# First part's plain values loaded as f32 on two other queues, plain heads first, and the first FFN tiles split by rows of x

## The chip, the cores and the metric

The kernel runs on one core of a Trainium2 chip. The metric is the device time of one execution in microseconds (us), given as the median of ten runs. One further execution was recorded by the hardware profiler; its rows are what this document reads. Five engines work side by side, each through its own queue of instructions in order: TensorE (PE, with its weight loads shown as PEld), VectorE (DVE), ScalarE (ACT), GpSimd (POOL) and SyncE (SP). Loads and stores (DMAs) are issued by an engine's queue and carried out by 16 DMA engines.

## The reference

Windowed attention over 8 batches, 8 heads, 576 tokens and 64 dimensions, followed by a feed-forward network (FFN) on the 4608 rows that it gives:

```python
scores = scale * np.matmul(q, k.transpose(0, 1, 3, 2))
rel = pos[:, None] - pos[None, :]
mask_plain = (rel >= 0) & (rel < 32)
mask_dil = (rel >= 0) & (rel < 128) & (rel % 4 == 0)
masks = np.stack([mask_plain if h < H // 2 else mask_dil for h in range(H)], axis=0)
attn = softmax(np.where(masks, scores, -1e9))
x = np.matmul(attn, v)            # (8, 8, 576, 64) -> rows of 512
h = np.maximum(x @ w_in, 0.0)     # 512 -> 2048
out = h * h @ w_out               # 2048 -> 512
```

Heads 0 to 3 are the *plain* heads (a window of 32 tokens), heads 4 to 7 the *dilated* ones (every fourth token of 128). Inputs and output are f32 in DRAM.

## The kernel before

**Pairs and parts.** Two heads share the 128 partitions, so there are four pairs e: 0 and 1 are plain, 2 and 3 dilated. The first two batches are worked in two *parts*: part 0 is tokens 0 to 255, part 1 the other 320. Only batch 0 (the "first" steps) and the first FFN tiles matter for the change.

**An order by hand.** The string PROGRAM (line 21) lists what is issued, in order. Everything up to the first bar runs before the first FFN group, what stands between two bars runs after one FFN group each. The engines follow this order each for its own instructions. The codes:

- `L0:q001` loads q and k of batch 0, part 0, pairs 0 and 1 (two DMAs, q then k); `q023` pairs 2 and 3; `q101`, `q123` the same for part 1. `L0:v0d` loads part 0's values of the dilated pairs (tile vds, two DMAs of 64 KB), `L0:v0p` those of the plain pairs (tile vbd, four DMAs of 32 KB as written), `v1dr` and `v1p` the values of part 1. `L0:i0` to `i3` load the four column pieces of w_in, `o0` to `o3` the four pieces of w_out, 512 KB each as written. `L1:...` are the loads of batch 1. All of these are issued by POOL and cast f32 to bf16 on the way. Loads by POOL use eight semaphores in turn, so each issue waits until the load eight before it has landed.
- `T` transposes q and k of a pair on PE (tiles of the PSUM pool ps_a, two buffers), `C` copies the result to SBUF (letter a: ACT takes q, or both; letter v: DVE; the plain pairs' k is always DVE's).
- `B` writes the mask as a large negative bias into a PSUM tile of the pool ps_f (four buffers), `S` adds the scores to it, `E` is the exponential on ACT.
- `P` multiplies the exponentials with the values, `D` sums them, `L` and `X` on ACT make the reciprocal of the sum (Ln, then Exp of its negative), `M` on DVE (line 620) writes the normalized result to xT. In part 0 a pair of pairs shares one L, X and M: `L20 X20 M20` is for pairs 2 and 3, `L00 X00 M00` for pairs 0 and 1.
- `W` and `w` are dummy matmuls on zeros (tile idle, line 465).

**vbd and its zeros.** vbd holds the values of a pair as a block diagonal: head 0's 64 columns on partitions 0 to 63, head 1's on 64 to 127, zeros elsewhere. ACT writes the zeros at the start (line 725), after it has issued the load of the constants mk (line 714); the loads of `v0p` fill the blocks.

**The FFN.** `ffn_groups` (line 645) makes the groups. Four tiles of 256 tokens come first (tile 0: tokens 0 to 255, tile 1: 256 to 511), then tiles of 512. A first-product step mm1(u, kts) multiplies the listed quarters kt of xT (kt is the pair e) with two of the 16 column blocks of w_in, accumulates in a tile of ps_f, and after the last quarter ACT applies Relu (line 679) and DVE squares (line 680). Blocks u = 0, 1 need i0, u = 2, 3 i1, u = 4, 5 i2, u = 6, 7 i3. In tile 0 each group is a whole mm1 of eight matmuls, in the order of quarters 2, 3, 0, 1; so the dilated pairs are wanted first. The *early* tiles (the four after tile 0) split their first groups: tile 1 works half of the quarters for u = 0 to 3 first and the others after, the rest three and one. The second product, `g2` (line 692), runs over tiles of 128 rows and four pieces of w_out, four matmuls a group; ACT copies the result to a tile osb (pool of three buffers) and SP stores it.

Line 808 sets the order of the first 16 groups. In `head`, 0 to 7 are tile 0's first-product groups, 16 to 23 tile 1's; before the change they run 0, 1, 2, 3, 16, 17, 18, 19, 4, 5, 20, 21, 6, 7, 22, 23. The next eight groups are tile 0's second product, pieces o0 and o1 of both row tiles, then o2 and o3.

Of the kernel before, what the change touches and what calls it, by code (L numbers as in the profile page):

```python
# [18 lines left out]


PROGRAM = (
    "L0:q001 L0:q023 L0:q101 L0:q123 L0:v0d L0:v0p L0:i0 L0:v1dr L0:i1 L0:v1p L0:i2 L0:i3 L0:o0 L0:o1 L0:o2 "
    "L0:o3 L1:q00123 z y L1:v0dp L1:q10123 L1:v1dpr w9 T00 C00a T10 C10a B00 B10 S00 E00 B20 S10 E10 B30 T20q "
    "B01 W2 T20k C20v T30 C30v B11 W1 S20 E20 W1 S30 E30 T01 C01v T11 C11v W1 S01 E01 T21 C21v B21 S11 E11 T31 "
    "C31v P20 P30 D20 D30 L20 X20 M20 P00 P10 D00 D10 L00 X00 M00 B31 S21 E21 S31 E31 W2 | | P21 P31 D21 D31 "
    "L21 X21 M21 L31 X31 M31 | | P01 P11 D01 D11 L01 X01 M01 L11 X11 M11 | | | | | | | | | | | | | m n | | | | "
    "| L2:q00123 L2:q10123 | 1q1 1q3 | 1q2 1k2 | 1k1 1v3 | 1a2 | 1v2 1k0 1q0 | 1o2 | 1a0 1a1 | 1k3 1o0 1o1 | "
    "1a3 1Q0 | 1K0 1o3 | 1Q1 1K1 | 1Q2 | 1b0 | | 1Q3 1K2 L2:vwpdr L3:q00123 L3:q10123 | L2:x | | 2q0 | | 2k0 "
# [35 lines left out]
def kernel(  # L64
# [9 lines left out]
    nc = tc.nc  # L74
    P = nc.NUM_PARTITIONS
    B, H, S, D = q.shape
    DM, DFF = moe_w_in.shape
# [3 lines left out]
    f32 = mybir.dt.float32  # L81
# [11 lines left out]
    NT = 512  # L93
# [7 lines left out]
    NF = DFF // P  # L101
# [7 lines left out]
    osb_pool = ctx.enter_context(tc.tile_pool(name="osb", bufs=3))  # L109

    ps_f = ctx.enter_context(tc.tile_pool(name="ps_f", bufs=4, space=bass.MemoryType.PSUM))
    ps_a = ctx.enter_context(tc.tile_pool(name="ps_a", bufs=2, space=bass.MemoryType.PSUM))
    ps_o = ctx.enter_context(tc.tile_pool(name="ps_o", bufs=1, space=bass.MemoryType.PSUM))
# [27 lines left out]
    idle = const.tile([P, 256], bf16, name="idle")  # L141
    kbd = const.tile([P, NE, NB, P], bf16, name="kbd")
    vbd = [const.tile([P, NE, NB, P], bf16, name=f"vbd{i}") for i in range(2)]
# [311 lines left out]
    first = {}  # L455
    sides = [slice(64 * hl, 64 * hl + 64) for hl in range(2)]

    def turn(n: int, cols: int):


        if "W" not in first:
            pool, nm = (ps_f, "pf") if ("P", 2, 0) in first else (ps_o, "po")
            first["W"] = pool.tile([P, 512], f32, name=nm)
        for _ in range(n):
            nc.tensor.matmul(
                first["W"][:, 0:cols], idle[:, 0:P],
                idle[:, 0:256].unsqueeze(1).broadcast_to([P, cols // 256, 256]), start=True, stop=True, skip_group_check=True
            )

    def first_step(code: str):  # L470
# [5 lines left out]
        what, e, part = code[0], int(code[1]), int(code[2])  # L476
        m0, n = MS[part], MN[part]
# [81 lines left out]
        elif what == "E":  # L559
            ps = first.pop(("S", e, part))  # L560
            nc.scalar.activation(pts[e][:, c : c + ps.shape[1]], ps, ACT.Exp, scale=SCALE)
        elif what == "P":
            if ("P", *pair) not in first:
                if pair in ((2, 0), (2, 1), (0, 1)):
                    od = ps_o.tile([P, 512], f32, name="po"), ps_d.tile([P, 512], f32, name="pd")
                else:
                    od = [ps_a.tile([P, 512], f32, name="pa") for _ in range(2)]
                first.pop("W", None)
                first["P", *pair] = od
            o, d = [x[:, y0 : y0 + w] for x in first["P", *pair]]  # L570
            o3, d3 = byr(o), byr(d)
            pt = pts[e]
            bl = blocks(0, e, part)
            y, dms = c, []
            for x, (i, r, q0, q1) in enumerate(bl):
                z = (q1 - q0) * (RES if r is None else 1)
                quads = dil and i < 8
                for rows in sides if quads else [slice(0, P)]:
                    if r is None:
                        to, rhs = o3[rows, :, q0 - m0 : q1 - m0], byr(pt[rows, y : y + z])  # L580
                    else:
                        to, rhs = o3[rows, r, q0 - m0 : q1 - m0], pt[rows, y : y + z]
                    if quads:
                        lhs = vds[0][rows, e - NE // 2, i // RES, D * (i % RES) : D * (i % RES) + D]
                    else:
                        lhs = vbd[0][:, e, i, :]
                    nc.tensor.matmul(
                        to, lhs, rhs, start=(x == 0 and y0 == 0), stop=(x == len(bl) - 1), skip_group_check=True
                    )
                if not dil:  # L590
                    dms.append((d3[:, :, q0 - m0 : q1 - m0], byr(pt[:, y : y + z])))
                y += z
            if dil and part == 0:
                dms.append((d, pt[:, 0:w]))
            elif dil:
                main = byr(pt[:, c : c + 448])
                dms += [(d3, main[:, :, 32:112]), (d3[:, :, 0:32], main[:, :, 0:32]),
                        (d3[:, :, 64:80], byr(pt[:, c + 448 : c + 512]))]
            first["D", e, part] = dms
        elif what == "D":  # L600
            dms = first.pop(("D", e, part))
            for x, (dd, rh) in enumerate(dms):
                nc.tensor.matmul(
                    dd, ones, rh, start=(x == 0 and y0 == 0), stop=(x == len(dms) - 1), skip_group_check=True
                )
        else:
            n = 512 if part == 0 else w
            if what == "L":
                first["X", e, part] = rec = r_pool.tile([P, 512], f32, name="rec")
                nc.scalar.activation(rec[:, 0:n], first["P", e, part][1][:, 0:n], ACT.Ln)  # L610
            elif what == "X":
                rec = first["X", e, part][:, 0:n]
                nc.scalar.activation(rec, rec, ACT.Exp, scale=-1.0)
            else:
                o, rec = first["P", e, part][0][:, 0:n], first.pop(("X", e, part))[:, 0:n]
                to = xT[:, e, RES * m0 : RES * m0 + n]
                if part == 0:
                    to = xT[:, e : e + 2, 0:w]
                    o, rec = [x.rearrange("p (e n) -> p e n", e=2) for x in (o, rec)]
                nc.vector.tensor_tensor(out=to, in0=o, in1=rec, op=ALU.mult)  # L620
# [24 lines left out]
    def ffn_groups(tk0: int, nt: int):  # L645

        early = 0 < tk0 <= 2 * NT
        h2 = h2_pool.tile([P, NF, NT], bf16, name="h2T")  # L650
        per = NT // nt
        kts = (0, 2, 1, 3) if tk0 >= NT else (2, 3, 0, 1)
        cut = 3 if tk0 >= NT else 2
        cur, acc = {}, {}

# [24 lines left out]
            nc.vector.tensor_tensor(out=hv, in0=hv, in1=hv, op=ALU.mult)  # L680

        def g1(i):
            if i < 2 and early:
                for u in (2 * i, 2 * i + 1):
                    mm1(u, kts[:cut])
            elif i < 4 and early:
                for u in (2 * i - 4, 2 * i - 3):
                    mm1(u, kts[cut:])
            else:
                mm1(i, kts)  # L690
# [21 lines left out]


    nc.scalar.dma_start(mk[:, :], mk_dram.ap())

    def zero_halves(t):
        nc.vector.memset(t[0:64, :, :, 64:128], 0.0)
# [49 lines left out]
    def run(code):  # L767
        if code == "y":
            for nm in "qk":
                nc.gpsimd.memset(staged(1, nm)[64:80, 0, :, :], 0.0)  # L770
                nc.gpsimd.memset(staged(2, nm)[64:80, 0, 0 : H // 2, :], 0.0)
        elif code == "z":
            nc.gpsimd.memset(vbd[1][0:64, :, :, 64:128], 0.0)
            nc.gpsimd.memset(vbd[1][64:128, :, :, 0:64], 0.0)
        elif code == "m":
            masks()
        elif code == "n":
            zero_halves(kbd)
            zero_halves(vbd[0][:, NE // 2 :, 0:8, :])
        elif code[0] in "wW":  # L780
            turn(int(code[1:]), 512 if code[0] == "w" else 256)
        elif code[0] in "TCBSEPDXM" or code[0] == "L" and code[2:3] != ":":
            first_step(code)
        elif code[0] != "L":
            step(int(code[0]), code[1:])
        else:
            b, what, part, which = int(code[1]), code[3], code[4:5], code[5:]
            if what == "q":
                load_qk(b, None if part == "w" else int(part), [int(e) for e in which])
            elif what == "x":  # L790
                cross_all(b)
            elif what == "v":
                load_v(b, [0, 1] if part == "w" else [int(part)], which)
            else:
                (load_w_in if what == "i" else load_w_out)(int(part))
# [9 lines left out]
        groups += ffn_groups(tk0, nt)  # L805

    head = groups[:G]
    groups[:NF] = [head[y] for y in (0, 1, 2, 3, 16, 17, 18, 19, 4, 5, 20, 21, 6, 7, 22, 23)]
    groups[NF:G] = [head[y] for y in (8, 9, 12, 13, 10, 11, 14, 15)] + head[24:32]
    for b in range(5, B):  # L810
        at = {"a": (-2, 8), "b": (0, 8), "o": (3, 8), "p": (6, 8), "v": (-4, 8)}
# [51 lines left out]
```

## Time and profile before

| what | value |
|---|---|
| median of 10 runs | 314.42 us (313.24 to 351.95) |
| the profiled execution | 313.35 us, of which the span of its instructions is 311.3 us |
| PE busy | 300.3 us (96%), 2532 matmuls |
| DVE busy | 193.9 us (62%) |
| ACT busy | 196.7 us (63%) |
| POOL busy | 96.5 us (31%) |
| first product, L668 | 132.7 us |
| second product, L700 | 131.1 us |
| granted TensorE clock | 1.00 |

The time counts a little more than the span of the instructions. Busy time of an engine says how much of the span it had an instruction running; what an engine waits for is read from the chain of waits and from the rows in order of time, where square brackets give the idle time ahead of an instruction and what ended it. In the windows view each engine has its busy time and a count of instructions, then come the granted clock, the mean busy share of the 16 DMA engines (over 1 when packets overlap) and GB/s. A row of the DMA queues gives packets, MB and the share of 16 engines over the span.

PE and the 16 DMA engines over the span, in 40 equal slices (the busy share in tenths):

```profile
PE   8889999999999999999999999999999999999994
DMA  7999999999999969999699976502200210121022
```

### The profile page before, as it was taken

What the parts mean: (1) busy time and instruction counts of PE and PEld (TensorE: products, weight loads), DVE (VectorE), ACT (ScalarE), POOL (GpSimd) and SP (SyncE); (2) the same over time, 40 slices, a digit from 0 to 9 for tenths busy, and PEclk for the clock granted to TensorE, in tenths of its full rate; (3) what the DMA queues carried; (4) which work ended last, traced back from release to release, by engine and by line L of the source; (5) the groups of instructions that cost most, each with busy time, mean ns of one, the idle gap of its engine ahead of it and who ended that gap; (6) DMA issues with size and microseconds to landing.
All of it is one profiled execution on the core that took longest, in us unless ns stands there. A gap on an engine that the chain in (4) does not pass through costs nothing.

```text
span 311.3 us, 6742 instructions
## 1 busy us (share of the span) xinstructions
PE 300.3 (96%) x2532; PEld 186.3 (60%) x2564; DVE 193.9 (62%) x631; ACT 196.7 (63%) x420; POOL 96.5 (31%) x142
## 2 busy tenths in 40 slices
PE   8889999999999999999999999999999999999994
PEld 3679746968755555565599555555555555445443
DVE  1435667998978879974898469946994334104400
ACT  7377738859878865785388547854786456226511
POOL 8889783665227255501451041000000000000000
PEclk9999999999999999999999999999999999999999
DMA  7999999999999969999699976502200210121022
GB/s 111 161 165 212 205 153 151 183 157 206 150 106 189 182 109 203 156 100 198 99 134 130 159 119 92 101 10 61 67 2 1 69 68 0 36 67 34 0 69 67
DMA packets 79808, 34.91 MB, mean 112 GB/s; under 512 B 49824, under 2 KB 74784, under 8 KB 79776
## 3 DMA queue, kind: packets, MB, share of 16 engines
q0 software_dynamic: 47680, 18.36, 53.9%
q1 hardware_dynamic: 31952, 15.93, 27.4%
q8 instruction: 20, 0.33, 0.5%
q10 hardware_dynamic: 144, 0.20, 0.2%
q14 instruction: 12, 0.10, 0.1%
HBM read 36.90 MB, written 9.44 MB: 149 GB/s over the span
## 4 chain that ended last, share of the span: by engine, by line
PE 78%; DMA 9%; ACT 5%; POOL 3%; DVE 2%; issue 2%; ACTq 0%; POOLq 0%
PE pf L700 35%; PE pf L668 33%; DMA w_out_sb<-in_moe_w_out_dram 5%; PE po L413 3%; PE pd L415 2%; DMA w_in<-in_moe_w_in_dram 2%; DMA qb<-in_q_dram 2%; PE pa L304 2%; PE pa L310 1%; ACT h2T L679 1%; ACT qT L248 1%; PE pa L235 1%; ACT rec L417 1%; ACT rec L418 1%; DVE xT L428 1%
## 5 line engine op out<-in xcount | busy, mean ns | idle before, releaser
L668 PE MATMUL pf<-xT,w_in 128*128 128x256 bf16 (+1 forms) x758 | 132.7, 325 | 2.4 <-DVE xT L620 0.7
L700 PE MATMUL pf<-w_out_sb,h2T 128*128 128x512 bf16 (+1 forms) x570 | 131.1, 373 | 1.7 <-ACT osb L706 0.5
L668 PEld LDWEIGHTS <-w_in 128*128 128x128 bf16 x768 | 82.3, 114 | 37.7 <-issue 2.2
L679 ACT ACTIVATE h2T<-pf 128x512 bf16<-128x512 f32 x144 | 83.7, 598 | 24.7 <-PE pf L668 23.9
L700 PEld LDWEIGHTS <-h2T 128*128 128x128 bf16 x592 | 54.3, 98 | 54.2 <-issue 1.0
L680 DVE TENSOR_TENSOR h2T<-h2T 128x512 bf16<-128x512 bf16 x144 | 58.1, 423 | 40.8 <-ACT h2T L679 39.3
L706 ACT COPY osb<-pf 128x512 f32<-128x512 f32 (+1 forms) x37 | 21.2, 573 | 42.4 <-PE pf L700 42.3
L428 DVE TENSOR_TENSOR xT<-po,rec 128x288 bf16<-128x288 f32 (+2 forms) x52 | 23.7, 456 | 30.7 <-ACT rec L418 30.2
L178 POOL DMA_DIRECT2D vbd<-in_v_dram x40 | 28.3, 725 | 44.4 <-PE pd L415 39.7
L417 ACT ACTIVATE rec<-pd 128x288 f32<-128x288 f32 (+2 forms) x52 | 21.4, 412 | 24.0 <-PE pd L415 22.3
L314 ACT ACTIVATE pt<-pa 128x352 bf16<-128x352 f32 (+6 forms) x56 | 27.6, 499 | 8.4 <-PE pa L310 4.7
L418 ACT ACTIVATE rec<-rec 128x288 f32<-128x288 f32 (+2 forms) x56 | 24.8, 444 | 1.8
L413 PEld LDWEIGHTS <-vbd 128*128 128x128 bf16 x286 | 16.8, 97 | 9.9 <-issue 0.7
L248 DVE COPY qT<-xx 64x288 bf16<-64x288 bf16 x80 | 19.6, 245 | 1.6 <-DMA xx<-qb 0.5
L252 DVE COPY kbd<-xx 64x288 bf16<-64x288 bf16 x40 | 18.8, 470 | 0.9 <-DMA xx<-kb 0.3
L191 POOL DMA_DIRECT2D vd<-in_v_dram x24 | 14.7, 627 | 14.7 <-DMA qb<-in_q_dram 7.5
L161 POOL DMA_DIRECT2D qb<-in_q_dram x18 | 13.0, 723 | 17.4 <-DMA xx<-qb 16.4
L413 PE MATMUL po<-pt,vbd 128*128 128x96 bf16 (+3 forms) x263 | 18.0, 199 | 0.3 <-DVE vbd L207 0.2
L415 PE MATMUL pd<-pt,mk 128*128 128x96 bf16 (+5 forms) x158 | 16.3, 204 | 0.0
L197 POOL DMA_DIRECT2D vbd<-in_v_dram x16 | 9.6, 606 | 13.8 <-PE pd L415 5.1
L161 POOL DMA_DIRECT2D kb<-in_k_dram x18 | 12.8, 713 | 1.2 <-issue 0.8
L304 PE MATMUL pa<-qT,kbd 128*128 128x96 bf16 (+2 forms) x146 | 12.2, 201 | 0.5 <-ACT qT L248 0.5
(82 smaller groups left out, 231.1 us busy)
## 6 DMA issues: line engine op xcount, KB each, us to landing
out_dram<-osb SPq DMA_DIRECT2D x18, 128.0 KB, 3.0
qb<-in_q_dram POOLq DMA_DIRECT2D x7, 320.0 KB, 6.7
kb<-in_k_dram POOLq DMA_DIRECT2D x7, 320.0 KB, 9.2
vd<-in_v_dram POOLq DMA_DIRECT2D x32, 64.0 KB, 5.8
w_in<-in_moe_w_in_dram POOLq DMA_DIRECT2D x4, 512.0 KB, 6.9
w_out_sb<-in_moe_w_out_dram POOLq DMA_DIRECT2D x4, 512.0 KB, 13.4
qb<-in_q_dram POOLq DMA_DIRECT2D x7, 256.0 KB, 7.1
kb<-in_k_dram POOLq DMA_DIRECT2D x7, 256.0 KB, 8.0
```

Of the source, the lines that this page charges most:

```text
L161: nc.gpsimd.dma_start(t[0:n, part, hs, :], src[b, hs, t0 : t0 + RES * n, :].rearrange("h (p r) d -> p h (r d)", r=RES))
L178: nc.gpsimd.dma_start(dst[rows, e, i0:i1, rows], v[b, 2 * e + hl, 64 * i0 : 64 * i1, :].rearrange("(i p) d -> p i d", p=64),)
L248: copy(qT[rows, e, :, m0 : m0 + n].rearrange("p (c j) m -> p j c m", j=2)[:, jj, :, :], src)
L314: nc.scalar.activation(pt[:, off : off + n], ps[:, 0:n], ACT.Exp, scale=SCALE)
L413: nc.tensor.matmul(oo, vb[:, e, i, :], rh, start=(x == 0), stop=(x == len(mms) - 1), skip_group_check=True)
L417: nc.scalar.activation(rec[:, 0:n], d[:, 0:n], ACT.Ln)
L418: nc.scalar.activation(rec[:, 0:n], rec[:, 0:n], ACT.Exp, scale=-1.0)
L428: nc.vector.tensor_tensor(out=tok, in0=o if o is o3 else o[:, 0:n], in1=rec if o is o3 else rec[:, 0:n], op=ALU.mult)
L668: nc.tensor.matmul(acc[u][:, nt * x + y0 : nt * x + y1], w_in_sb[piece][:, kt, c0 : c0 + 509 : 4], xT[:, kt, t0 : t0 + y1 - y0], start=(kt ...
L679: nc.scalar.activation(hv, acc[u][:, :].rearrange("p (x n) -> p x n", x=per), ACT.Relu)
L680: nc.vector.tensor_tensor(out=hv, in0=hv, in1=hv, op=ALU.mult)
L700: nc.tensor.matmul(cur[m][:, c0:c1], h2[:, f, P * m : P * m + P], w_out_sb[:, f, c0:c1], start=(f == 0), stop=(f == NF - 1),)
```

## The change

The program's first segments are written anew:

```diff
-    "L0:q001 L0:q023 L0:q101 L0:q123 L0:v0d L0:v0p L0:i0 L0:v1dr L0:i1 L0:v1p L0:i2 L0:i3 L0:o0 L0:o1 L0:o2 "
-    "L0:o3 L1:q00123 z y L1:v0dp L1:q10123 L1:v1dpr w9 T00 C00a T10 C10a B00 B10 S00 E00 B20 S10 E10 B30 T20q "
-    "B01 W2 T20k C20v T30 C30v B11 W1 S20 E20 W1 S30 E30 T01 C01v T11 C11v W1 S01 E01 T21 C21v B21 S11 E11 T31 "
-    "C31v P20 P30 D20 D30 L20 X20 M20 P00 P10 D00 D10 L00 X00 M00 B31 S21 E21 S31 E31 W2 | | P21 P31 D21 D31 "
+    "L0:q001 L0:q023 L0:q101 L0:q123 L0:v0d L0:i0 L0:v1dr L0:i1 L0:v1p L0:i2 L0:i3 L0:o0 L0:o1 L0:o2 L0:o3 "
+    "L1:q00123 z y L1:v0dp L1:q10123 L1:v1dpr w9 T00 C00a T10 C10a h B00 B10 S00 E00 B20 S10 E10 B30 W2 T20q "
+    "W3 T20k C20v T30 C30v W3 S20 E20 W3 S30 E30 P00 P10 D00 D10 L00 X00 T01 C01v M00 T11 C11v B01 B11 P20 P30 "
+    "D20 D30 L20 X20 M20 W3+11 S01 T21 C21a T31 C31v E01 S11 E11 | B21 S21 E21 | B31 S31 E31 P21 P31 D21 D31 "
     "L21 X21 M21 L31 X31 M31 | | P01 P11 D01 D11 L01 X01 M01 L11 X11 M11 | | | | | | | | | | | | | m n | | | | "
```

`L0:v0p` is gone from POOL's list. Its values are loaded as they are, f32, into a buffer of the osb pool: two DMAs by SP (pair 0) and two by ACT (pair 1), issued right after mk and before ACT's zero copies. The new code `h`, two DVE copies, casts them into vbd:

```diff
     nc.scalar.dma_start(mk[:, :], mk_dram.ap())
+    plain = osb_pool.tile([P, DM], f32, name="osb")[:, :].rearrange("p (e i d) -> p e i d", e=2, d=D)
+    for e, engine in enumerate((nc.sync, nc.scalar)):
+        for hl, rows in enumerate(sides):
+            engine.dma_start(
+                plain[rows, e, :, :], v[0, 2 * e + hl, 0:256, :].rearrange("(i p) d -> p i d", p=64)
+            )
...
+        elif code == "h":
+            for rows in sides:
+                nc.vector.tensor_copy(vbd[0][rows, 0:2, 0:4, rows], plain[rows, :, :, :])
```

`turn`, the dummy matmuls, can now add its zeros into a score tile that already holds its bias (`W3+11`: three of them into the tile of pair 1, part 1), and otherwise uses one tile of ps_o. P00 takes its two PSUM tiles from ps_f in place of ps_a:

```diff
-                    od = [ps_a.tile([P, 512], f32, name="pa") for _ in range(2)]
+                    pool, nm = (ps_a, "pa") if part else (ps_f, "pf")
+                    od = [pool.tile([P, 512], f32, name=nm) for _ in range(2)]
```

In the FFN, tile 0 takes the quarters in the order 0, 1, 2, 3, and tiles 0 and 1 split their first two groups by rows of x (quarters): the first group has the first two quarters of u = 0 and 1, the second the other two. Tile 1 is no longer one of the early tiles. Head 16 stays fifth, 4 and 5 come before 17, 18 and 19:

```diff
-        early = 0 < tk0 <= 2 * NT
+        early = NT <= tk0 <= 2 * NT
-        kts = (0, 2, 1, 3) if tk0 >= NT else (2, 3, 0, 1)
+        kts = (0, 2, 1, 3) if tk0 >= NT else (0, 1, 2, 3) if tk0 == 0 else (2, 3, 0, 1)
...
         def g1(i):
-            if i < 2 and early:
+            if i < 2 and tk0 < NT:
+                for u in range(2):
+                    mm1(u, kts[2 * i : 2 * i + 2])
+            elif i < 2 and early:
...
-    groups[:NF] = [head[y] for y in (0, 1, 2, 3, 16, 17, 18, 19, 4, 5, 20, 21, 6, 7, 22, 23)]
+    groups[:NF] = [head[y] for y in (0, 1, 2, 3, 16, 4, 5, 17, 18, 19, 20, 21, 6, 7, 22, 23)]
```

## The prediction

> **What bounds the kernel now.** I read the page's chain of waits first: TensorE (PE) holds 78% of it, DMA 9%. PE is the bound over the span, and a change to the first 41 us can give only what PE gets back there. So the second view is the same chain for 0 to 41 us (start, length, what):
>
> ```profile
> 5.08 5.62 DMA qb<-in_q_dram
> 10.70 0.28 issue
> 10.99 6.41 DMA w_in<-in_moe_w_in_dram
> ...
> 22.28 17.04 DMA w_out_sb<-in_moe_w_out_dram
> 39.32 0.04 issue
> 39.36 1.67 PE pf L700 x7
> ```
>
> Up to 39.36 us the chain is loading: a q load, the first w_in piece (i0), the last w_out piece (o3). The third view is POOL in order of time, since POOL issues all of these loads:
>
> ```profile
> 7.59 0.64 POOL L178 DMA_DIRECT2D vbd<-in_v_dram  x1
> 8.73 1.91 POOL L178 DMA_DIRECT2D vbd<-in_v_dram  x3 [0.50 <-DMA kb<-in_k_dram]
> 10.99 0.76 POOL L752 DMA_DIRECT2D w_in<-in_moe_w_in_dram  x1 [0.35 <-DMA qb<-in_q_dram]
> ...
> 17.68 1.34 POOL L178 DMA_DIRECT2D vbd<-in_v_dram  x2 [1.23 <-DMA w_in<-in_moe_w_in_dram]
> 18.99 1.55 POOL L752 DMA_DIRECT2D w_in<-in_moe_w_in_dram  x2
> ```
>
> The first two rows are the four loads that the change takes out. The brackets show that each issue waits for the landing of the one eight before it: i0 is POOL's 15th load and waits for the 7th. The fourth view is PE around its first FFN matmul, and how dense it is after:
>
> ```profile
> 16.48 0.39 PE L465 MATMUL pf<-idle 128*128 128x256 bf16 x2
> 17.45 0.41 PE L668 MATMUL pf<-xT,w_in 128*128 128x256 bf16 x2 [0.57 <-DMA w_in<-in_moe_w_in_dram]
> 18.20 1.69 PE L668 MATMUL pf<-xT,w_in 128*128 128x256 bf16 x14 [0.35 <-DVE xT L620]
> ```
> ```profile
> 17.40:26.20 8.80, 8.10 (x114) 7.37 (x115) 4.36 (x9) 6.48 (x15) 8.37 (x11) 1.00 1.30 173
> 26.20:34.80 8.60, 8.60 (x79) 8.60 (x79) 4.29 (x11) 6.24 (x11) 8.56 (x9) 1.00 1.09 216
> ```
>
> PE meets i0 and the normalized rows (xT) almost at once, then has 79 matmuls in 8.60 us without a hole (0.109 us each; second and third figure: length, PE busy). Between 17.4 and 26.2 it loses 1.2 us before L668: 0.7 to xT, 0.6 to i0 by the groups of that stretch.
>
> **The change, part by part.**
>
> *Four issues leave POOL.* i0's issue can move from 10.99 to 7.59 (it is then the 11th load and waits only for the 3rd, landed by 2.61 + 4.7 = 7.3). But its data stand behind other loads. By issue plus time to landing: the second v0d lands at 6.93 + 5.3 = 12.2, the last of the four at 10.02 + 4.4 = 14.4, i0 at 17.4. So the four cost 2.2 us of queue. In that stretch one packet of the instruction queue also ran, 2.1% of 16 engines over 2.6 us, which is 0.9 us on the one engine that carried it; it stays, so 1.3 are saved. Besides, i0 took 3.0 us behind the loads ahead of it, and i1, issued long before its turn, 20.9 - 18.5 = 2.4; issued early, i0 saves up to 0.6 more. Together 1.9 us. Bounds: 1.3, and 3.4 if i0 keeps its 6.4 us from the earlier issue. Behind it the order is unchanged: v1p's third issue waits for i0 in both programs, so i2's issue (18.99) moves with i0, and i2, which lands 4.2 us after the last v1p where i3 follows i2 in 2.6, may win a little more. I take 2.1 for i2 (landed 18.99 + 7.2 = 26.2) and o3 (39.3); bounds 1.3 and 3.4.
>
> *The same values come back as f32 on SP and ACT.* 256 KB, 1024 packets of 256 bytes. SP is free (its first issue is at 41.03). What they take from q and k behind them is not shown, so two bounds:
>
> ```profile
> q1 hardware_dynamic: 31952, 15.93, 27.4%
> ```
> ```profile
> 1.00:2.00 1.00, 0.93 (x3) 0.38 (x4) 0.01 (x1) 1.00 (x1) 0.75 (x1) 1.00 0.19 32
> 2.00:3.00 1.00, 1.00 (x4) 0.35 (x3) 0.00 (x0) 0.99 (x2) 1.00 (x3) 1.00 0.58 168
> ```
>
> Queue q1 (the SP stores and transposes) took 27.4% of 16 x 311.3 us for 31952 packets: 43 ns each, so 1024 cost 2.7 us on 16 engines; by bytes (15.93 MB in 85 us) 1.4 us. Against that the engines are idle for 0.81 + 0.42 = 1.2 us between 1 and 3 us (second-last figure: DMA share). So the delay lies between 0 and 1.5 us. I take 0.6, nearer the byte price, since these packets are smaller than q1's mean of 500 bytes. Net: i0 lands 1.9 - 0.6 = 1.3 earlier, at 16.1; i2 and o3 1.5 earlier, at 24.7 and 37.8.
>
> A rule of the Trainium skill speaks against this part: "DMA: Bandwidth & Descriptors", section "Issuing engines are not separate DMA queues", says that DMAs from SP, ACT and POOL run on the same 16 engines, so spreading the issue saves only issue time. The share of 1.46 to 1.91 between 10 and 12 us agrees that the engines are full there, while the 0.19 and 0.58 above show room at the start. By the rule alone the 1.3 us come back as 1.3 us, and the sum below would end within 0.1 us of nothing; by the rows it ends at 0.8.
>
> *ACT issues two of the four* before its zero copies (L725, 2.04 to 4.96). mk's issue took 0.34 us, SP's transposes 1.3 to 1.5; so ACT's copies end between 4.96 and 7.0, where its next work starts at 5.86 after 0.89 idle. I take the mk row: hidden. At the other end the front is 1.2 us late.
>
> *VectorE (DVE) casts (h)*: two copies of 64x512 f32. Rows: a 128x512 bf16 copy took 0.42, the L620 product on f32 0.69; so 0.8 to 1.4 us. They fall into this hole, between 7.02 and 8.86:
>
> ```profile
> 8.86 0.42 DVE L503 COPY xx<-pa 128x512 bf16<-128x512 bf16 x1 [1.84 <-PE pa L496]
> ```
>
> Hidden. Without the hole they would delay C20v, which stands behind them, and with it S20.
>
> *Plain products first.* P00 to D10 (0.63 us, 14.82 to 15.45 before) start after S30 at 10.2, and their L, X, M (0.60 + 0.63 + 0.69) end near 13.1 instead of 18.15. P20 to D30, T and S of the rest follow: 4.2 us of PE from 10.2, plus an instruction stall of 0.80 that PE had at 13.6, so PE is ready for the FFN near 15.2, 0.9 before i0. The dummy matmuls (W) go from 7 to 12, 0.5 us, all ahead of that wait. The cover is this 0.9; if it goes, the front costs one for one.
>
> *FFN by rows, and S21, S31 moved behind the first FFN groups.* The 0.7 wait for xT goes. PE from i0 on: group 0 0.87 (8 x 0.109), B21 S21 0.52 (half of 15.45 to 16.48), group 1 0.87, B31 S31 0.52, P21 to D31 1.4 (19.82 to 21.2), groups 2 and 3 1.74, P01 to D11 1.0, then head 16 0.87. New wait: E31 stands in ACT behind two Relu (L679, 0.60 each) and E21, and P31 with all PE work behind it waits for E31: 0.45. Sum 8.2: PE reaches head 4 at 16.1 + 8.2 = 24.3. Head 4 needs i2, formerly after eight groups, now after five: i2 is there at 24.7, a new wait of 0.4 (none before: head 4 ran 15 matmuls after 26.19, near 27.8).
>
> From there 11 groups are left, 88 x 0.109 = 9.6: the second product starts at 34.3 (34.81 before). Twenty matmuls of 0.216 (from 34.81 on) reach o3's group at 38.6, and o3 has been there since 37.8. Before, PE stood at 39.36. **Gain 0.8 us.** After 41 us the order is unchanged and PE-bound, so I carry it to the end.
>
> The profiled execution took 313.35 us (span 311.3), the median was 314.42; the sum says 312.6 for the one, so 313.6 for a median.
>
> **Rivals.**
> 1. *The early loads cost nothing and i0 keeps its latency*: 7.59 + 6.4 = 14.0, i2 3.4 earlier at 22.8. Then PE's own 15.2 starts the FFN; 15.2 + 8.2 + 9.6 + 4.3 = 37.3 against 39.36: 2.0 less, 312.4. For: the idle DMA at the start, and a share of 58 GB/s between 12 and 13 us where i0 could have run. Against: v0d's landing at 12.2.
> 2. *The load work only moves* (delay 1.5, saving 2.1): i2 at 25.6, head 4 starts there, 25.6 + 9.6 + 4.3 = 39.5: 314.5, no change. For: the 2.7 us by packets. Against: room in the first 3 us.
> 3. *Slower: h waits for a late load.* DVE is in order; h stands ahead of C20v, and so of S20, S30 and everything up to the FFN. If SP's and ACT's packets alternate with the q and k backlog until 11.5, h ends at 12.7 instead of 8.2, C20v starts 3.8 late, PE is ready at 19.0: 19.0 + 8.2 + 13.9 = 41.1, 1.7 more: 316.1. It costs from a landing at 8.6 on (8.86 - 1.2 + 0.9 of cover) and has eaten the whole gain at 9.4. For: 256-byte pieces behind 512-byte ones. Against: mk, issued at 0.78, landed after 2.3 us.
>
> **How the numbers follow.** Forecast 0.51, rival 1 0.27, rival 2 0.12, rival 3 0.10. Predicted is the forecast's 313.6. Its own range, with the delay between 0 and 1.3, is 312.9 to 314.6; the whole range reaches to rival 1 and towards rival 3: 312.2 to 315.4. About 0.5% (1.6 us) is what a measurement of this kernel tells from no change. Faster by more: most of rival 1 and a corner of the forecast, 0.27. Slower by more: rival 3 and a little else, 0.11. Within: 0.62.
>
> **What would show it.** i0 issued near 7.6 and landed near 16 (near 14: rival 1; near 17: rival 2). First L668 matmul near 16.1 with a wait for w_in, not for xT. A wait for w_in near 24.5 at head 4. No wait for w_out near 38.6. h between 7 and 8.9, C20v near 8.9 (later: rival 3). PE's first product of q, at 5.02 before, shows the delay by the early loads. I am wrong if head 4 doesn't wait and the second product still starts near 34.8, or if PE differs after 41 us.

## The result, and the profile after

| | before | after |
|---|---|---|
| median | 313.71 us (49 runs) | 316.88 us (14 runs, 315.58 to 529.46) |
| ratio | | 1.0092, interval 1.0068 to 1.0117 |
| profiled execution, its span | 313.35 us, 311.3 us | 315.88 us, 314.1 us |
| PE busy | 300.3 us | 302.9 us |
| granted TensorE clock, mean | 1.00 | 0.989 |

The change made the kernel 0.9% slower: 3.2 us in the medians, 2.5 us between the two profiled executions. The ratios in this text are not the quotients of the medians: runs in a slow state are left out of them, here the one of 529.46 us, at a mean clock of 0.558. The forecast for the median was 313.6 us (0.8 below the 314.42 of the first ten runs), its range ended at 315.4; for the profiled execution it was 312.6.

The last row of the table is the key. On the page of the changed kernel the rows of 40 equal slices (7.85 us each) show where the clock was low:

```profile
PE   6999999999999999999999999999999999999994
PEclk9599999999999999999999999999999999999999
```

In the second slice, 7.9 to 15.7 us, PE is fully busy while the mean granted clock is between 0.5 and 0.6. Before, this row showed no such slice. The chain of waits from 0 to 45 us (start, length, what) no longer runs through w_in and w_out:

```profile
1.99 5.02 DMA kb<-in_k_dram
...
7.05 0.33 PE pa L497 x8
...
9.72 0.43 PE po L467 x2
...
10.50 0.76 PE po L467 x3
...
19.16 1.00 PE pf L670 x8
...
26.82 10.48 PE pf L670 x96
```

It starts with the load of the first pair's k, and from 7.05 us on it is PE's own work, dummy matmuls (L467) among it, until the FFN begins. PE in order of time:

```profile
1.07 4.02 PE L467 MATMUL po<-idle 128*128 128x512 bf16 x9 [1.07 <-DVE idle L731]
5.94 0.31 PE L497 MATMUL pa<-mk,qb 64*64 64x64 bf16 x8 [0.84 <-DMA qb<-in_q_dram]
7.05 0.31 PE L497 MATMUL pa<-mk,kb 64*64 64x64 bf16 x8 [0.80 <-DMA kb<-in_k_dram]
...
10.43 0.82 PE L467 MATMUL po<-idle 128*128 128x256 bf16 x3
...
17.28 0.49 PE L467 MATMUL pf<-idle 128*128 128x256 bf16 x3
...
19.09 1.07 PE L670 MATMUL pf<-xT,w_in 128*128 128x256 bf16 x8
...
23.14 0.46 PE L589 MATMUL pa<-pt,vd 64*64 64x32 bf16 x16 [0.30 <-ACT pt L562]
...
26.65 10.65 PE L670 MATMUL pf<-xT,w_in 128*128 128x256 bf16 x96
37.14 1.03 PE L705 MATMUL pf<-w_out_sb,h2T 128*128 128x512 bf16 x3
```

The brackets say that PE stood still for 0.84 us until q, and for 0.80 us until k had landed. The transposes of q and k began at 5.02 and 5.44 us before, and begin at 5.94 and 7.05 us now. The first FFN product starts at 19.09 (17.45 before), the second at 37.14 (34.81 before). From the second product's start to the end of the span it is 277.0 us, against 276.5 before. So 2.3 of the 2.8 us in span are lost before the second product, and 1.6 of them already at the first. Of the rest, 0.27 us is a wait of PE at 49.81 us for values of the second batch (vbd, copied by DVE at L207) that the kernel before does not have; what makes it stays open.

The windows view shows what the two short waits did. Its columns are those of the prediction's windows: stretch, length, busy time of PE, PEld, DVE, ACT and POOL, then the granted clock. The stretches are cut where the recorded clock changes. After:

```profile
5.13:8.55 3.42, 1.55 (x44) 1.12 (x44) 0.74 (x3) 1.08 (x4) 2.96 (x5) 1.00 1.41 192
8.55:11.96 3.41, 3.41 (x53) 2.02 (x48) 1.21 (x4) 0.93 (x2) 2.62 (x5) 0.50 1.42 194
11.96:15.37 3.41, 3.41 (x42) 2.32 (x38) 0.54 (x2) 0.77 (x2) 2.13 (x3) 0.50 1.33 199
```

Before, in the stretches that belong to its own change of clock:

```profile
5.62:9.03 3.41, 3.14 (x84) 2.16 (x81) 0.93 (x3) 1.57 (x4) 2.91 (x6) 1.00 1.23 151
...
15.86:19.27 3.41, 2.49 (x50) 2.00 (x51) 1.39 (x2) 2.72 (x6) 2.18 (x4) 1.00 1.35 197
```

After one stretch of 3.4 us in which PE was busy for 1.55 us, the clock is at half for two such stretches, 6.8 us. PE looks full there, but it works slowly: the same three dummy matmuls take 0.82 us at 10.43 and 0.49 us at 17.28. Only this one execution of the changed kernel was traced. Of its thirteen runs in the ratio eight have a mean clock of 0.973 to 0.989, and five one of 0.998 to 1.000 although they took 316.14 to 317.16 us; the last section says why such a mean does not rule out a half clock at the start.

What the change was to do on POOL did happen:

```profile
8.04 0.77 POOL L763 DMA_DIRECT2D w_in<-in_moe_w_in_dram  x1
...
16.60 1.33 POOL L178 DMA_DIRECT2D vbd<-in_v_dram  x2 [2.45 <-DMA w_in<-in_moe_w_in_dram]
...
37.31 0.61 POOL L178 DMA_DIRECT2D vbd<-in_v_dram  x1 [1.95 <-DMA w_out_sb<-in_moe_w_out_dram]
```

i0 is issued at 8.04 instead of 10.99 and has landed at 16.3 (the issue at 16.60 waited for it; 17.4 before), and o3 at 37.0 (39.3 before). DVE in order of time has the cast h where it was expected, with no wait for a load ahead of it:

```profile
8.48 1.00 DVE L790 CAST vbd<-osb 64x512 bf16<-64x512 f32 x2
```

### The profile page after: what moved, and what is told of

Same layout as the page of the kernel before. It is cut to its first block, busy times and chain, and to the rows that moved or that the text cites. A ratio compares the mean times of both kernels' runs of the same rounds, so it can differ in the third digit from the quotient of the medians.

```text
span 314.1 us, 6761 instructions
## 1 busy us (share of the span) xinstructions
PE 302.9 (96%) x2539; PEld 188.1 (60%) x2571; DVE 195.3 (62%) x632; ACT 197.4 (63%) x421; POOL 94.0 (30%) x138
## 4 chain that ended last, share of the span: by engine, by line
PE 86%; ACT 6%; DVE 3%; issue 2%; DMA 2%; POOL 0%; ACTq 0%; POOLq 0%
PE pf L670 37%; PE pf L705 36%; PE po L413 3%; PE pd L415 2%; PE pa L304 2%; DMA kb<-in_k_dram 2%; ACT h2T L681 2%; PE pa L310 1%; ACT qT L248 1%; PE pa L497 1%; DVE kbd L252 1%; PE po L467 1%; PE pf L557 1%; ACT rec L417 1%; PE pa L235 1%
## 5 line engine op out<-in xcount | busy, mean ns | idle before, releaser
L681 ACT ACTIVATE h2T<-pf 128x512 bf16<-128x512 f32 x144 | 83.6, 597 | 23.2 <-PE pf L670 22.6
L428 DVE TENSOR_TENSOR xT<-po,rec 128x288 bf16<-128x288 f32 (+2 forms) x52 | 23.7, 456 | 30.9 <-ACT rec L418 30.3
L178 POOL DMA_DIRECT2D vbd<-in_v_dram x36 | 25.7, 731 | 55.4 <-PE pd L415 48.2
L417 ACT ACTIVATE rec<-pd 128x288 f32<-128x288 f32 (+2 forms) x52 | 21.5, 413 | 24.0 <-PE pd L415 22.9
L161 POOL DMA_DIRECT2D qb<-in_q_dram x18 | 13.1, 729 | 23.1 <-DMA xx<-qb 21.7
L415 PE MATMUL pd<-pt,mk 128*128 128x96 bf16 (+5 forms) x158 | 16.3, 203 | 0.0
L161 POOL DMA_DIRECT2D kb<-in_k_dram x18 | 12.9, 715 | 1.0 <-DMA kb<-in_k_dram 0.7
L197 POOL DMA_DIRECT2D vbd<-in_v_dram x16 | 9.7, 614 | 10.0 <-PE pd L415 7.4
## 6 DMA issues: line engine op xcount, KB each, us to landing
w_out_sb<-in_moe_w_out_dram POOLq DMA_DIRECT2D x4, 512.0 KB, 12.7
```

The lines of the kernel that those rows point to most:

```text
L161: nc.gpsimd.dma_start(t[0:n, part, hs, :], src[b, hs, t0 : t0 + RES * n, :].rearrange("h (p r) d -> p h (r d)", r=RES))
L178: nc.gpsimd.dma_start(dst[rows, e, i0:i1, rows], v[b, 2 * e + hl, 64 * i0 : 64 * i1, :].rearrange("(i p) d -> p i d", p=64),)
L417: nc.scalar.activation(rec[:, 0:n], d[:, 0:n], ACT.Ln)
L428: nc.vector.tensor_tensor(out=tok, in0=o if o is o3 else o[:, 0:n], in1=rec if o is o3 else rec[:, 0:n], op=ALU.mult)
L681: nc.scalar.activation(hv, acc[u][:, :].rearrange("p (x n) -> p x n", x=per), ACT.Relu)
```

## The experiments

**Theory.** The early loads take DMA time from exactly the two loads that PE needs first. PE is idle for 1.6 us in one stretch of 3.4 us, the clock goes to half, and PE is late for the FFN. **Rivals.** The time goes to the new order or to the dummy matmuls W; or the loads themselves cost it, whatever the clock does; or h, its casts and ACT's issues stand in the way. Each ratio below is to the kernel before, timed on the same chip (its medians there: 313.61 to 314.03 us).

**Fewer dummies alone, in the kernel before.** Five opening dummies instead of nine; nothing else is changed.

```diff
-    "... z y L1:v0dp L1:q10123 L1:v1dpr w9 T00 C00a ..."
+    "... z y L1:v0dp L1:q10123 L1:v1dpr w5 T00 C00a ..."
```

> The kernel before with 5 instead of 9 opening dummy matmuls, nothing else: PE is then idle from 3.2 to 5.0 us. If idle time near the start alone halves the clock (theory 1): a granted clock of 0.5 over some 3.4 to 14 us of the first 25, first L668 matmul 1 to 4 us later than 17.45, time 315 to 318, with no change to any load. If the loads or the order are what costs (theory 2): clock full and time 313.7 as before.

Measured: 316.56 us, ratio 1.0072 (1.0043 to 1.0101). PE in order of time:

```profile
4.70 0.42 PE L496 MATMUL pa<-mk,qb 64*64 64x64 bf16 x8 [1.31 <-DMA qb<-in_q_dram]
...
20.56 0.38 PE L668 MATMUL pf<-xT,w_in 128*128 128x256 bf16 x2
```

No load is added and no dependence changed, and yet the FFN starts at 20.56 instead of 17.45. The eight small transposes take 0.42 us, as they do at the half clock of the start; in the changed kernel, at full clock, they took 0.31. The clock's first recorded rise is at 19.8 us. So a front at half clock is by itself worth 2.9 us (316.56 against 313.69 on that chip), nearly the loss of the changed kernel. It is not quite the same event: here four dummies are missing as well as a gap being open, and the clock had not risen yet; in the changed kernel it was full from 5.1 us and fell at 8.5.

**The gap filled, in the changed kernel.** Thirteen opening dummies instead of nine; all early loads stay.

```diff
-    "... L1:v1dpr w9 T00 C00a T10 C10a h B00 ..."
+    "... L1:v1dpr w13 T00 C00a T10 C10a h B00 ..."
```

> The changed kernel with 13 instead of 9 opening dummy matmuls (0.43 us each at half clock), so that PE stays busy until q and k of the first pair land (5.9 and 7.0 us there). Theory 1 (the loss is the half clock from 8.5 to 15.4 us, brought on by PE's idle time between 5.1 and 8.3): the clock stays full, the first L670 matmul comes near 16.8 instead of 19.1 us, time near 313.7, 2.3 below the changed kernel. Theory 2 (the loss is the late k and the order on PE, the clock is incidental): first L670 near 19, time near 316. Rival 3 (extra dummies only delay the first transposes): later than the changed kernel.

Measured: 312.68 us, ratio 0.9969 (0.9958 to 0.9981): 4.2 us below the changed kernel and 0.3% below the kernel before.

```profile
1.07 5.31 PE L467 MATMUL po<-idle 128*128 128x512 bf16 x13 [1.07 <-DVE idle L731]
6.31 0.31 PE L497 MATMUL pa<-mk,qb 64*64 64x64 bf16 x8
6.64 0.31 PE L497 MATMUL pa<-mk,kb 64*64 64x64 bf16 x8
...
16.04 1.06 PE L670 MATMUL pf<-xT,w_in 128*128 128x256 bf16 x8
...
34.12 6.21 PE L705 MATMUL pf<-w_out_sb,h2T 128*128 128x512 bf16 x28
```

q is transposed later than in the changed kernel (6.31 against 5.94), and everything after is earlier, because PE does not stand still and the clock stays full. From 6.64 to the first FFN product it takes 9.4 us; in the changed kernel, from 7.05, it takes 12.0. The two profiled executions differ by 3.4 us (315.88 and 312.49), of which 2.6 are in this stretch and 0.4 come from a k that landed earlier in this one.

**Without the early loads, in the changed kernel.** The tile plain is zeroed instead of loaded, so part 0's plain heads of batch 0 come out as zeros; order, h and dummies are as in the changed kernel.

```diff
-    for e, engine in enumerate((nc.sync, nc.scalar)):
...
-            engine.dma_start(plain[rows, e, :, :], v[0, 2 * e + hl, 0:256, :]...)
+    nc.vector.memset(plain[:, :, :, :], 0.0)
```

> The changed kernel without its four early loads of plain values: VectorE sets their tile to zero at the start and h casts zeros, so part 0's plain heads of batch 0 come out as zero; all else is as in the changed kernel. Theory 1 (the early loads push the first q and k back by 1.2 and 1.6 us, and all else follows from that): q lands near 4.7, k near 5.4, clock full after the start, first L670 near 15 to 16, time 311.5 to 312.5. Theory 2 (the new order on PE is itself slower): q and k as before, but first L670 not before 17.5 and time not under 314.

Measured: 312.26 us, ratio 0.9963 (0.9931 to 0.9996).

```profile
5.02 0.34 PE L497 MATMUL pa<-mk,qb 64*64 64x64 bf16 x8
5.21 0.31 PE L497 MATMUL pa<-mk,kb 64*64 64x64 bf16 x8
...
15.51 1.06 PE L670 MATMUL pf<-xT,w_in 128*128 128x256 bf16 x8
...
33.55 6.21 PE L705 MATMUL pf<-w_out_sb,h2T 128*128 128x512 bf16 x28
```

With nine dummies and the new order, q and k are worked at 5.02 and 5.21, and the clock holds. So the early loads are what opens the gap. In the traces k landed at 6.6 to 7.6 us in the seven kernels that issue them on two queues at the start, and at 5.2 to 5.4 in the six that have none there. With the gap filled and the clock kept they cost 0.4 us (312.68 against 312.26, with intervals that overlap); with the gap open, 4.2 more (316.88 against 312.68).

**The loads alone, in the kernel before.** v0p is taken out, the early loads and h are put in, the old order stays; first with nine dummies, then with thirteen.

```diff
-    "... L0:v0d L0:v0p L0:i0 ..."
+    "... L0:v0d L0:i0 ..."
+    for e, engine in enumerate((nc.sync, nc.scalar)): ...
```

> The kernel before with the new loads and casts alone: v0p off POOL's list, four early f32 loads on SP and ACT, h after C10a; program order and FFN order as before. Theory 1: q and k land 1.2 and 1.6 us late as in the changed kernel; with the clock halved for a window or two the first L668 comes at 18 to 19 and time is 315 to 316.5; with the clock kept it is 313 to 314. Theory 2 (order on PE): 313 or less, since i0 comes about 1 us earlier and the old order stands.

> The kernel before with the new loads and casts and 13 opening dummies, program order and FFN order as before. Theory 1 (clock): full clock, so at least 3 us below the 317.7 of the same without the 4 more dummies. If the new order on PE is needed to turn the earlier loads into time: front 1.2 us later than before, the normalized rows at 18 to 19, time 314 to 315. If the early loads alone carry the gain: 312.7 as with the new order.

Measured: 317.65 us with nine (ratio 1.0123, 1.0091 to 1.0155, four runs) and 314.53 us with thirteen (1.0021, 1.0001 to 1.004). PE with nine:

```profile
6.09 0.31 PE L496 MATMUL pa<-mk,qb 64*64 64x64 bf16 x8 [1.15 <-DMA qb<-in_q_dram]
7.09 0.31 PE L496 MATMUL pa<-mk,kb 64*64 64x64 bf16 x8 [0.69 <-DMA kb<-in_k_dram]
...
22.22 2.13 PE L668 MATMUL pf<-xT,w_in 128*128 128x256 bf16 x16
```

The same two waits and, without the new order, a clock at half from 8.1 to 21.7 us. Filling the gap gives 3.1 us back here as well. But even then the loads bring nothing under the old order. PE with thirteen:

```profile
19.05 1.69 PE L668 MATMUL pf<-xT,w_in 128*128 128x256 bf16 x14 [0.77 <-DVE xT L620]
```

i0 is no longer what ends last; the wait for xT is. In the trace of the new order with thirteen dummies PE has no such wait.

**The order alone.** The changed kernel's order with v0p loaded by POOL as before, without the early loads and h.

```diff
-    "... L0:v0d L0:i0 ..."   ... C10a h B00 ...
+    "... L0:v0d L0:v0p L0:i0 ..."   ... C10a B00 ...
```

> The changed kernel's order with the loads of the kernel before (v0p cast by POOL, no early loads, no h). q and k land as before at 4.7 and 5.4. P00 now stands ahead of T01 in PE's order and waits for v0p, which lands near 14.4: PE idle from 10.2 on, then 4.2 us of work: first L670 near 18.6 and time near 314.5 with the clock kept, 316 or more if this idle time halves it. If the order needs nothing of the loads: under 313.7.

Measured: 318.49 us, ratio 1.0141 (1.008 to 1.0202, four runs).

```profile
13.45 0.71 PE L589 MATMUL pf<-pt,vbd 128*128 128x96 bf16 x8 [3.10 <-DMA vbd<-in_v_dram]
...
20.61 1.89 PE L670 MATMUL pf<-xT,w_in 128*128 128x256 bf16 x8
```

P00 comes 3.1 us too early for its values, and the clock is at half from 14.4 to 24.6 us: eight matmuls of the first product take 1.89 us instead of 1.06. With nine dummies, neither the order nor the loads gain anything alone.

**The dummies W.** W2 and the three W3 left out between S00 and P00; first with nine opening dummies, then with thirteen.

```diff
-    "... B30 W2 T20q W3 T20k C20v T30 C30v W3 S20 E20 W3 S30 E30 P00 ..."
+    "... B30 T20q T20k C20v T30 C30v S20 E20 S30 E30 P00 ..."
```

> The changed kernel without the 11 dummy matmuls W2 W3 W3 W3 among T20 to S30 (W3+11 stays). At half clock they hold PE for 2.4 us of the front. If they stand on the path: first L670 near 17, time near 314. If they are what ends the half clock (at 15.4 us), the half clock lasts a window of 3.4 us longer and time is equal or up to 1 us worse. If neither, 316.

> The changed kernel with 13 opening dummies and without the 11 dummies W2 W3 W3 W3. At full clock these take 1.2 us of PE on the way to the first L670 (16.04 us with 13 openers, where w_in landed at 15.4). If the clock holds: first L670 at 15.5, time 312.2. If they keep the clock up: half clock after 9 us, time 314 to 316.

Measured: 315.56 us with nine (1.0065, 1.0036 to 1.0095), 312.83 us with thirteen (0.998, 0.9942 to 1.0017). The first is 1.3 us below the changed kernel, but the intervals overlap. Its profiled execution was the longest of its runs (318.50 us) and still ran at half clock at the first product:

```profile
19.55 1.90 PE L670 MATMUL pf<-xT,w_in 128*128 128x256 bf16 x8
```

The second equals the 312.68 us with the W, with a wider spread (312.1 to 317.93). In its profiled execution (314.77 us) thirteen dummies were not enough:

```profile
7.65 0.31 PE L497 MATMUL pa<-mk,kb 64*64 64x64 bf16 x8 [0.86 <-DMA kb<-in_k_dram]
```

k had landed later than with the W kept (7.6 against 6.6 us), and the clock was at half from 8.7 to 15.5. What the W are worth stays open. They are not the loss: the changed kernel with thirteen dummies keeps all of them and takes 312.68 us.

**Nothing in front of q and k, the loads held back.** With nine dummies, the four loads go to SP behind a small ACT copy at 3.1 us, h behind C30v, and the plain products behind T11.

```diff
-    for e, engine in enumerate((nc.sync, nc.scalar)):
...
+            if es.start == 0 and hl == 0:
+                nc.scalar.copy(plain[:, :, 0, 0:1], idle[:, 0:2].unsqueeze(2))
+                for x in range(4):
+                    part = sides[x % 2]
+                    nc.sync.dma_start(
+                        plain[part, x // 2, :, :], v[0, x, 0:256, :].rearrange("(i p) d -> p i d", p=64)
+                    )
-    "... C10a h B00 ... C30v W3 ... E30 P00 P10 D00 D10 L00 X00 T01 C01v M00 T11 C11v ..."
+    "... C10a B00 ... C30v h W3 ... E30 T01 C01v T11 C11v P00 P10 D00 D10 L00 X00 M00 ..."
```

> The changed kernel with 9 opening dummies, whose four early loads are all issued by SP and held back: a small ACT copy into their tile stands behind ACT's first zero copy (ends at 3.2 us), so their packets start near 4.5 instead of 2 us. h moves behind C30v, and P00 to M00 behind T11. If the early loads hurt only through the first q and k: q lands near 4.7 and k near 5.4 as before, clock full, first L670 near 15.5, time 312.0 to 312.5. If the same delay only moves to the second q and k pair: T20k starts 0.5 to 1 us late and first L670 near 16.3, time near 313. If h now waits for a late load: C01v late, first L670 at 17 or later, time 314.

Measured: 315.25 us, ratio 1.0012 (0.9976 to 1.0047), runs from 313.15 to 318.79; the profiled one took 317.15, so the trace shows one of the longer runs, and this version is not told from the kernel before. q and k were worked at 4.79 and 5.33 us. The engines in order of time:

```profile
10.95 0.42 DVE L792 CAST vbd<-osb 64x512 bf16<-64x512 f32 x1 [1.21 <-DMA osb<-in_v_dram]
12.50 0.42 DVE L792 CAST vbd<-osb 64x512 bf16<-64x512 f32 x1 [1.13 <-DMA osb<-in_v_dram]
12.95 0.32 DVE L511 COPY xx<-pa 128x320 bf16<-128x320 bf16 x1
...
12.98 0.49 PE L589 MATMUL pf<-pt,vbd 128*128 128x96 bf16 x8 [1.73 <-DVE vbd L792]
```

In this execution the mechanism of the third rival is there: h waits for its loads, C01v behind it and PE wait for h, and then the clock falls too (14.7 to 21.6 us). Moving the loads back moved the gap back.

**All four loads on SP, thirteen dummies.**

```diff
-    for e, engine in enumerate((nc.sync, nc.scalar)):
+    for e, engine in enumerate((nc.sync, nc.sync)):
```

> The changed kernel with 13 opening dummies and all four early loads on SP (0.72 us per issue, so the last is issued near 2.9 instead of 1.5 us). If the loads' number ahead of k is what delays it: k lands near 6.2 instead of 6.6 to 7.0, PE's first transposes follow the dummies at 6.3 without a hole, time 312.3. If all four still run ahead of k: as with two queues, 312.7. The fourth load may land near 8.5; then h, at 8.4 in that kernel, waits, and time is 313 or more.

Measured: 312.62 us, ratio 0.994 (0.9914 to 0.9966). The four issues start between 0.75 and 2.89 us, so the last loads are later, and the second cast of h on DVE waits:

```profile
8.54 0.72 DVE L790 CAST vbd<-osb 64x512 bf16<-64x512 f32 x1 [0.53 <-DMA osb<-in_v_dram]
```

The cast is done at 9.3, and DVE still idles before C20v at 9.6. k landed at 6.1 us, earlier than in any of the seven kernels with the loads on two queues, but this is one execution. The median is that of the version with two queues (312.68) within the noise. Of the versions that load all their values these two have the lowest medians.

**Controls: thirteen dummies in the kernel before, and the old FFN split in the best version.**

```diff
-        early = NT <= tk0 <= 2 * NT
+        early = 0 < tk0 <= 2 * NT
...
-            if i < 2 and tk0 < NT:
-                for u in range(2):
-                    mm1(u, kts[2 * i : 2 * i + 2])
-            elif i < 2 and early:
+            if i < 2 and early:
...
-    groups[:NF] = [head[y] for y in (0, 1, 2, 3, 16, 4, 5, 17, 18, 19, 20, 21, 6, 7, 22, 23)]
+    groups[:NF] = [head[y] for y in (0, 1, 2, 3, 16, 17, 18, 19, 4, 5, 20, 21, 6, 7, 22, 23)]
```

> The kernel before with 13 instead of 9 opening dummies, nothing else: a control. If the gain of the changed kernel with 13 dummies (312.7) is that of its loads and order, this is not faster than the kernel before: the transposes start near 6.0 instead of 5.0, the front is 0.5 to 1.2 us late, time 314 to 315. If the dummies alone bring it (a steadier clock): 312.7 here too.

> The changed kernel with 13 opening dummies and the FFN of the kernel before: tiles 0 and 1 no longer split by rows, the first 16 groups in the old order (tile 0 still takes the plain quarters first). If the split by rows carries a part of the gain: group 0 waits for the dilated rows (M20), time 0.3 us or more above 312.7. If loads and plain products first carry it all: 312.5 to 312.9. With i2 wanted three groups later nothing can be won there, since no wait for w_in was left.

Measured: 313.34 us for the first (0.9993, 0.998 to 1.0007), which is no change and not the loss that was expected: in the median the dummies alone bring nothing. The second gave 313.70 us (1.0003, 0.9991 to 1.0014), 1.0 us above the version with the new split. Its PE waits where the old split has the second tile's late quarters:

```profile
26.86 8.79 PE L670 MATMUL pf<-xT,w_in 128*128 128x256 bf16 x79 [0.30 <-DVE xT L622]
```

From the first to the second product it takes 18.67 us, against 18.08 with the new split. Between the two profiled executions (313.87 and 312.49 us) 0.6 of 1.4 us lies there; the other 0.8 are there already at the first product, with a k worked at 7.47 instead of 6.64. How much of the 1.0 us in the medians is the order of the groups is not separated.

## Why the prediction was wrong

**The failed step** is "PE is ready for the FFN near 15.2, 0.9 before i0", with the sentence on its cover. The 15.2 was counted at full clock from a start that the early loads were assumed not to move. Measured from the traces: k's transposes start at 7.05 instead of 5.44, so 1.6 late; from there PE needs 12.0 us instead of the 9.8 that the working implies (15.2 - 5.44), 2.3 more (12.04 less 9.76), for most of it at half clock. Less the 0.9 of cover that is 1.6 + 2.3 - 0.9 = 3.0 us: the first product came at 19.1 where 16.1 was forecast. This is nearly the whole error for the profiled execution (315.88 - 312.6 = 3.3). That the clock, and not just the later k, makes the 2.3 is shown by the thirteen dummies: with the same loads the stretch takes 9.4 us. The kernel with five dummies agrees: no load is added, and the FFN is 3.1 us late. A small term was miscounted as well: the program has 14 dummies W, not 12, which is 0.2 us more at 0.109 each.

**Delay by the early loads, "between 0 and 1.5 us. I take 0.6".** As a mean over the queue it held: by the landings in the trace i0 came at 16.3 (16.1 forecast), and the second v0d 0.3 us later than before. But the delay is not spread evenly. q of the first pair landed 1.2 us later and k 1.6, and the loads behind caught up: the DMA share was 1.41 from 5.1 to 8.5 us, where it had been 1.23 from 5.6 to 9.0. The working priced the average and named the delayed q as a sign of it, not as a cost.

**i2 and o3.** i2 landed at 23.7 and o3 at 37.0, 1.0 and 0.8 us earlier than forecast. So the wait of 0.4 for i2 at head 4 was not there: the 96 matmuls from 26.65 on have no gap.

**FFN by rows.** Right in the main. From first to second product 18.05 us were measured (19.09 to 37.14) and 18.2 forecast, but the 18.2 held the 0.4 for i2, so its other terms were short by 0.25; the wait of P31 for E31 is there with 0.30 us in the row at 23.14 (0.45 forecast), and the wait for xT is gone.

**h, and ACT's issues.** h took 1.00 us from 8.48 (0.8 to 1.4 forecast) and was hidden: DVE idles for 2.17 us behind it before C20v, and for 0.96 with thirteen dummies, where all comes earlier. ACT's two issues took 0.72 us each, twice the row that was taken, inside its bounds; the zero copies ended at 5.57, before k was there. Both cost nothing. **After 41 us** the forecast carried the difference to the end unchanged. From the second product to the end it is 277.0 us, against 276.5 before and 276.6 with thirteen dummies; of the three only the changed kernel has the wait at 49.81.

**The rivals.** None of them named the mechanism. The time fell where the prediction had put 0.11 (slower by more than 1.6 us), but not for the reason that it gave. The forecast's own gain of 0.8 is near what the change gives once the clock is kept: 1.0 us (313.71 to 312.68). That is partly luck: in that kernel i0 landed at 15.4 us and the first product started at 16.04 without a wait for it, so PE and not i0 set the start. The third rival stood on the right ground, early loads against q and k, but put the price on h. With the loads held back its wait was there, and that the second cast ended at 12.9 us, where the rival had said 12.7, is chance, since the loads were issued later and h stood further back.

## What to carry to other kernels

Price an idle gap of PE not only by its length: ask what it does to the clock, and price what follows at half clock too. At the front of this kernel, among small transposes, two waits of 0.8 us within 3.4 us were enough. Early loads, even on other queues, delayed the first loads most (q by 1.2 us and k by 1.6, the second v0d by 0.3), so the delay has to be set against what waits for those, not against an average. Dummy matmuls at the start are sized to the landing of the first operand; when an edit moves that landing, they have to be moved with it, and with room to spare: in the execution where k landed at 7.6 us, thirteen were too few.

## What the runs showed of the hardware

**How little idle time turns the clock down.** Between its recorded changes the granted clock holds for whole multiples of 3.41 us. In the stretch of 3.41 us just ahead of a fall to half, or in one that no fall followed, PE was busy for:

| kernel | fall at | PE busy in the 3.41 us before |
|---|---|---|
| order alone | 14.4 us | 0.82 |
| loads held back | 14.7 us | 1.38 |
| loads alone | 8.1 us | 1.54 |
| the changed kernel | 8.5 us | 1.55 |
| thirteen dummies, no W | 8.7 us | 2.14 |
| before (the least of its front, 15.9 to 19.3 us) | none | 2.49 |
| before, thirteen dummies (the least of its front, 19.5 to 22.9 us) | none | 2.38 |
| the changed kernel, at its end (308.9 to 312.3 us) | none | 1.52 |
| before, at its end (306.0 to 309.4 us) | none | 1.91 |
| without the early loads, at its end | 308.9 us | 0.98 |

So PE need not be idle for a whole stretch, and its busy time alone does not decide. At the front, where most of what runs are matmuls of 64x64 and 80x80, 2.14 of 3.41 us was too little. At the end, where only matmuls of 128x256 are left, 1.52 us in the changed kernel was enough: the clock stays at 1.00 in the idle stretch behind it.

```profile
308.92:312.33 3.41, 1.52 (x14) 1.12 (x12) 0.00 (x0) 0.37 (x1) 0.00 (x0) 1.00 0.22 77
312.33:314.10 1.77, 0.00 (x0) 0.00 (x0) 0.00 (x0) 0.00 (x0) 0.00 (x0) 1.00 0.00 0
```

What else counts than busy time, these runs do not show. The Trainium skill, "TensorE: Matmul & The Clock Gate", section "Part 1: The HAM clock gate (the "warmup" mystery)", has the same length of window, free-running, and says that the clock halves after at least one idle window. The runs agree with the length; for the fall they show, at the front, windows that were far from idle.

**How long it stays down.** Two stretches in the changed kernel (6.8 us), three with the order alone (10.2), four with the loads alone (13.7), although PE was busy for 3.18 to 3.41 of 3.41 us in each of these four. The section cited gives one busy window as enough. Much of what ran were matmuls of 64x64 and 80x80 with their weight loads; whether it is their small size that delayed the rise was not tried.

**What the clock's row does not show.** Before the first recorded change the row reads 1.00. In the kernel with five dummies it does so up to 19.8 us, while eight transposes took 0.42 us instead of 0.31. The length of a known matmul tells the clock there. The kernel without W and with nine dummies has the same program as the changed kernel up to its first W; there eight transposes took 0.42 us at 5.96, and the first recorded rise is at 23.2 us. So in one execution the clock rose early and fell again, and in another it had not risen. The changed kernel's five runs with a mean of 0.998 to 1.000 may be of the second kind; no trace shows it.
